# Second mixture: slots' outcome and result in two parts of columns, 256 and 128

## The chip, the core and the metric

The kernel runs on one core of a Trainium2 chip. Its time is counted in microseconds (us) of the device for one execution. A core has TensorE (PE, whose weight loads are listed apart as PEld), VectorE (DVE), ScalarE (ACT), GpSimd (POOL) and SyncE (SP, which here only issues transfers), and 16 DMA engines that move data between HBM and the core's memory. TensorE's products go to PSUM, in banks of 512 float32 columns; ACT and DVE copy them from there to SBUF.

## What is computed

A linear-attention recurrence gives 3072 rows of 384 numbers. A first mixture sends each row through one of eight experts. A second mixture, with which this case deals, collects the rows in 32 slots (8 experts with 4 slots each), runs each slot through its expert, and gives every row a weighted sum of the 32 slots' outcomes:

```python
def _moe2_ref(x, phi, w1, w2):
    logits = x @ phi
    ...
    slot_input = d.T @ x
    slot_input = slot_input.reshape(E, S_per_e, D)
    for e in range(E):
        h = np.maximum(slot_input[e] @ w1[e], 0.0)
        slot_out[e] = h @ w2[e]
    slot_out = slot_out.reshape(n_slots, D)
    c = logits - logits.max(1, keepdims=True)
    c = np.exp(c)
    c /= c.sum(1, keepdims=True) + 1e-09
    return (c @ slot_out).astype(np.float32)
```

Here D is 384, E is 8, S_per_e is 4 and the hidden size is 1024. w1 and w2 of this mixture are called v1 and v2 in the kernel.

## The kernel before

The span falls into three stretches: the attention (to about 110 us), the first mixture (to about 290 us), and the second mixture's end, which is all that the change touches.

The weights v1 and v2 are 32 tiles of 768 KB, fetched in a fixed order by SP: sixteen tiles of v1, then sixteen of v2 (`VORD`). They go wherever room comes free. The last eight tiles of v2, `V[2, 1, 0]` to `V[2, 1, 7]`, take the slots of tiles of v1, so SP waits until the hidden layer has read those (L215).

`experts` is the stage of the slots. The experts are in two groups of four (g = 0, 1), and the four of one group work side by side on TensorE, each in its own 32 columns of the array. `first(g, n)` computes half n of the hidden layer (L215) and ACT applies relu (L217). `turn(g, n)` transposes it in four blocks (L224), and DVE copies them out (L225). `last(g, n)` multiplies by four tiles of v2 and adds into the one bank `sop`, 384 columns (L233): for each tile four instructions side by side, which are a quad below; float32 products run as two passes over the columns, so that a tile costs two quads in the trace, and a call of `last` eight. Every one of the sixteen tiles of v2 must be in before `sop` is complete. Then ACT copies `sop` to `sst`, rounded (L256), and DVE adds what the rounding lost in other rows (L257).

`weights` makes the combining weights of 1024 rows on DVE and ACT, and `turned` (called by `ctt(c)`) transposes those of 512 rows on TensorE (L289) for ACT to copy to `ct` (L290).

`combine` makes the result. For c = 0 to 5, each standing for 512 rows, and for b = 0 to 3, one matmul multiplies `ct` by `sst` (L298: 128 rows of 384 columns), ACT or DVE copies it to `ob` (L300, L302), and SP writes `ob` out. For c = 0 there are three writes (L304 twice with one b each, L305 with two); for the others one of 768 KB (L305). A row of the result is 1536 bytes in a piece, and so are the packets of these writes. `ctt(c + 2)` follows each `combine(c)`.

The engines PE, DVE, ACT and POOL run in the order in which the code is written (`manual_schedule`), each on its own; waits between them are put in where one needs another's result or buffer.

Of the kernel before, what the change touches and what calls it, by code (L numbers as in the profile page):

```python
# [19 lines left out]
P = 128  # L20
# [184 lines left out]
def experts(nc, cn, ew, ez, pe, spx, rw, V, after=lambda blk: None):  # L205
    ident = cn["ident"]
    hs, ht = {}, {}

    def first(g, n, between=lambda: None):
        if n == 0:  # L210
            hs[g] = ew.tile([P, 2, HF], F32, tag="hs", bufs=1, name=f"hs{g}")
        hp = pe.tile([P, HF], F32, tag="h", name=f"ehp{g}_{n}")
        for k in range(3):
            for j in range(4):
                nc.tensor.matmul(hp[32 * j : 32 * j + 32, :], spx[:, g, k, j, :], V[1, 4 * g + j, n][:, k, :], start=(k == 0), stop=(k == 2))  # L215
        between()
        nc.scalar.activation(hs[g][:, n, :], hp, AF.Relu, scale=rw.scale[:, 0:1])  # L217

    def turn(g, n):
        if n == 0:  # L220
            ht[g] = ew.tile([P, 8, P], F32, tag="ht", bufs=2, name=f"ht{g}")
        tp = pe.tile([P, 4, P], F32, tag="a", name=f"htp{g}_{n}")
        for f in range(4):
            nc.tensor.transpose(tp[:, f, :], hs[g][:, n, f * P : (f + 1) * P], ident)  # L224
        nc.vector.tensor_copy(  # L225
            ht[g][:, 4 * n : 4 * n + 4, :].rearrange("p f (j q s) -> p (f j) q s", j=4, q=4),
            tp.rearrange("p f (j o s) -> p (f j) o s", j=4, o=4)[:, :, 0:1, :].to_broadcast([P, 16, 4, 8]),
        )

    def last(g, n):  # L230
        for f in range(4 * n, 4 * n + 4):
            for j in range(4):
                nc.tensor.matmul(sop[32 * j : 32 * j + 32, :], ht[g][:, f, 32 * j : 32 * j + 32], V[2, g, f][:, j, :], start=(g == 0 and f == 0), stop=(g == 1 and f == 7))  # L233

    sop = pe.tile([P, DM], F32, tag="so", name="sop")
    first(0, 0)
    after(0)
    first(0, 1)
    after(1)
    turn(0, 0)  # L240
    first(1, 0, lambda: turn(0, 1))
    after(2)
    first(1, 1)
    after(3)
    last(0, 0)
    turn(1, 0)
    turn(1, 1)
    after(4)
    last(0, 1)
    after(5)  # L250
    after(6)
    last(1, 0)
    after(7)
    last(1, 1)
    sst = ez.tile([P, DM], F32R, name="sst")
    nc.scalar.copy(sst, sop)  # L256
    nc.vector.scalar_tensor_tensor(sst, sst.bitcast(F32), rw.low[:, 0:1], sop, op0=ALU.mult, op1=ALU.add)  # L257
    return sst


def weights(nc, lp, ez, lt, p, cx=None):
# [21 lines left out]
    return cx
# [9 lines left out]
def combine(nc, po, pool, tag, bufs, sst, ct, c, out):  # L293
    ob = pool.tile([P, B, DM], F32, tag=tag, bufs=bufs, name=f"ob{c}")
    o = out.rearrange("(b c t) d -> c t b d", b=B, c=NC_)[c]
    for b in range(B):
        op = po.tile([P, DM], F32, tag="o", name=f"op{c}_{b}")
        nc.tensor.matmul(op, ct[:, b, :], sst, start=True, stop=True)  # L298
        if b % 2 == (c > 0):
            nc.scalar.copy(ob[:, b, :], op)  # L300
        else:
            nc.vector.tensor_copy(ob[:, b, :], op)  # L302
        if c == 0 and b < 2:
            nc.sync.dma_start(out=o[:, b : b + 1], in_=ob[:, b : b + 1])  # L304
    nc.sync.dma_start(out=o if c else o[:, 2:4], in_=ob if c else ob[:, 2:4])  # L305


def second(tc, cn, dsb, lt, v1, v2, out):
    nc = tc.nc
    with tc.tile_pool(name="ew", bufs=1) as ew, tc.tile_pool(name="vp", bufs=1) as vp, tc.tile_pool(name="pe", bufs=1, space=PSUM) as pp:  # L310
        pe = Banks(a=[(pp, "a", 2)], so=[(pp, "so", 1)], h=[(pp, "h", 2)], o=[(pp, "o", 3)])
# [161 lines left out]
def tile_main(ctx, tc, rk, kv, wu, wcat, phi, w1, w2, v1, v2, r_in, k_in, v_in, w_in, u_in, wcn, out, dbg=None, force=False):  # L473
# [874 lines left out]
    if True:  # L1348
# [314 lines left out]
```

## Time and profile before

| | us |
|---|---|
| median of 3 runs | 350.69 (348.82 to 350.75) |
| the profiled execution, its device time | 347.19 |
| the span of its trace | 345.1 |
| TensorE, busy | 321.6 (93%) |
| VectorE, busy | 228.9 (66%) |
| ScalarE, busy | 159.5 (46%) |
| HBM read and written | 74.49 MB and 10.10 MB, 245 GB/s over the span |

Times in the trace count from the span's start. A row of the timeline gives start, duration, engine, line, operation, what is written and read, and in brackets the idle time before it and what ended it. A row of windows gives, for a stretch, each engine's busy time and instructions, the clock granted to TensorE as a share of full speed, the mean busy share of the 16 DMA engines (it can pass 1, since packets overlap), and the GB/s that they moved. Busy shares over the whole span say little here: only the last 40 us are touched.

### The profile page before, as it was taken

How to read it: one execution, taken by the hardware profiler on the slowest of the kernel's cores; microseconds unless marked ns; L12 is line 12 of the kernel's file. 1: busy time of each engine (PE TensorE's matmuls, PEld its weight loads, DVE VectorE, ACT ScalarE, POOL GpSimd, SP SyncE). 2: the span in 40 equal slices, each digit the busy share in tenths (PEclk: the TensorE clock that was granted, in tenths of full speed). 3: DMA queues.
4: the chain of work that ended last, by engine and by line, in shares of the span. 5: the costliest groups of instructions: out<-in, count | busy, mean ns of one | idle time of the engine just before them, and what ended most of it. 6: DMA issues, size and time to landing. Idle time of an engine off the chain costs nothing. (4 is left out here: it accounts for less than half of the span.)

```text
span 345.1 us, 10483 instructions
## 1 busy us (share of the span) xinstructions
PE 321.6 (93%) x4351; PEld 262.9 (76%) x4351; DVE 228.9 (66%) x512; ACT 159.5 (46%) x351; POOL 139.5 (40%) x181
## 2 busy tenths in 40 slices
PE   8999997999998998999999999999999999999850
PEld 8666785777766683999999999998999998634440
DVE  6657688696978966776674847675685846417650
ACT  2344452445543545554655546564655543221360
POOL 4867684686843554804323242525224102200000
PEclk9999998999999999999999999999999999999995
DMA  7996567485777965898788787778866649479496
GB/s 230 293 242 206 166 201 228 128 283 184 236 230 243 385 229 185 265 308 312 262 284 289 247 272 267 264 270 274 317 189 225 225 128 330 151 268 371 142 349 206
DMA packets 45735, 85.29 MB, mean 247 GB/s; under 512 B 3838, under 2 KB 26672, under 8 KB 45680
## 3 DMA queue, kind: packets, MB, share of 16 engines
q1 hardware_dynamic: 43024, 80.63, 70.9%
q0 software_dynamic: 2128, 3.74, 4.0%
q8 instruction: 36, 0.59, 0.7%
q10 hardware_dynamic: 528, 0.16, 0.2%
q14 instruction: 19, 0.16, 0.1%
HBM read 74.49 MB, written 10.10 MB: 245 GB/s over the span
## 5 line engine op out<-in xcount | busy, mean ns | idle before, releaser
L1259 PE MATMUL hp<-xhl,wa 128*128 128x240 f32 x192 | 46.1, 282 | 0.2 <-issue 0.2
L996 DVE TENSOR_TENSOR wa<-w,wa 128x768 fp32r<-128x768 f32 x32 | 30.5, 956 | 22.4 <-ACT wa L1008 22.0
L1284 PE MATMUL yp<-wb,hh 128*128 128x384 f32 x128 | 45.2, 353 | 0.0
L1260 PE MATMUL hp<-xhl,wa 128*128 128x240 f32 x192 | 44.6, 275 | 0.0
L1285 PE MATMUL yp<-wb,hh 128*128 128x384 f32 x128 | 43.0, 336 | 0.0
L1286 PE MATMUL yp<-wb,hl 128*128 128x384 f32 x128 | 42.9, 335 | 0.0
L1190 POOL DMA_INDIRECT xg<-x_d,idg x16 | 19.8, 1238 | 50.7 <-DVE x L1292 38.1
L630 POOL TENSOR_TENSOR pd<-rkb 112x512 f32<-112x512 f32 x24 | 31.0, 1293 | 22.4 <-PE ud L658 17.1
L1314 POOL DMA_INDIRECT lt_d<-lsr,ids x16 | 17.7, 1107 | 50.5 <-ACT xhl L1249 28.4
L1259 PEld LDWEIGHTS hp<-xhl,wa 128*128 128x128 f32 x192 | 36.2, 189 | 0.5 <-ACT dsbv L135 0.5
L1260 PEld LDWEIGHTS hp<-xhl,wa 128*128 128x128 f32 x192 | 36.2, 189 | 0.0
L706 DVE COPY_PREDICATED at<-ih,ud 128x512 f32<-128x512 int32 x24 | 17.7, 738 | 26.7 <-ACT us L687 16.5
L996 DVE TENSOR_TENSOR wb<-w,wb 128x768 fp32r<-128x768 f32 x32 | 30.5, 953 | 2.0 <-ACT wb L1008 1.7
L1008 ACT CAST wb<-w 128x768 fp32r<-128x768 f32 x32 | 26.8, 838 | 9.5 <-PE yp L1286 5.5
L1269 ACT ACTIVATE hh<-hp 128x480 fp32r<-128x480 f32 x32 | 18.3, 572 | 21.9 <-PE hp L1262 19.3
L745 PE MATMUL yp<-at,kvt 64*48 64x64 f32 (+3 forms) x800 | 26.6, 248 | 1.4 <-DVE at L706 0.8
L1270 DVE SCALAR_TENSOR_TENSOR hl<-hp,hh 128x480 fp32r<-128x480 f32 x32 | 20.9, 655 | 9.6 <-ACT hh L1269 9.2
L1008 ACT CAST wa<-w 128x768 fp32r<-128x768 f32 x32 | 26.9, 840 | 0.0
L1284 PEld LDWEIGHTS yp<-wb,hh 128*128 128x128 f32 x128 | 24.0, 188 | 3.5 <-issue 3.5
L1262 PE MATMUL hp<-xhl,wa 128*128 128x240 f32 x192 | 26.7, 275 | 0.0
L745 PEld LDWEIGHTS yp<-at,kvt 64*48 64x48 f32 (+1 forms) x800 | 21.1, 122 | 7.3 <-PE wp L499 2.2
L648 PE MATMUL sc<-rks 48*64 48x128 f32 (+1 forms) x768 | 21.9, 250 | 4.6 <-DVE at L697 4.6
(346 smaller groups left out, 697.7 us busy)
## 6 DMA issues: line engine op xcount, KB each, us to landing
w<-in_w_dram SPq DMA_DIRECT2D x32, 768.0 KB
v<-in_v_dram SPq DMA_DIRECT2D x29, 768.0 KB
rkb<-in_rk_dram SPq DMA_DIRECT2D x24, 448.0 KB
kvt<-in_kv_dram SPq DMA_DIRECT2D x24, 384.0 KB
x_d<-x SPq DMA_DIRECT2D x5, 768.0 KB
out_dram<-ob SPq DMA_DIRECT2D x5, 768.0 KB
x<-in_v_dram SPq DMA_DIRECT2D x2, 768.0 KB
x_d<-x SPq DMA_DIRECT2D x2, 384.0 KB
```

Source lines behind the costliest of these rows:

```text
L630: nc.gpsimd.tensor_mul(t["pd"], rkt[:, 0], rkt[:, 1])
L648: nc.tensor.matmul(sc[c0 : c0 + HT, g, blocks(p, z), :], ks[r0 : r0 + D, p, HT * z : HT * z + HT], rs[r0 : r0 + D, p, HT * z :], start=Tru ...
L745: nc.tensor.matmul(d, kvt[s0 : s0 + HT, 1, h * D : h * D + m], w, start=(c == ph == z == 0), stop=(ph == z == 1))
L996: nc.vector.tensor_sub(lv, sl, hv.bitcast(F32))
L1008: nc.scalar.copy(hv, sl)
L1259: nc.tensor.matmul(hp[:, f, 0:ROOM], hi[:, k, fs], xh[:, k, 0:ROOM], start=(k == 0 and f == 0), stop=False)
L1260: nc.tensor.matmul(hp[:, f, 0:ROOM], lo[:, k, fs], xh[:, k, 0:ROOM], start=False, stop=False)
L1262: nc.tensor.matmul(hp[:, f, 0:ROOM], hi[:, k, fs], xl[:, k, 0:ROOM], start=False, stop=(k == 2 and f == 1))
L1270: nc.vector.scalar_tensor_tensor(l, p, 0.0, h.bitcast(F32), op0=ALU.max, op1=ALU.subtract)
L1284: nc.tensor.matmul(YP[e][bl], hh[:, f, bs], hi[:, f, :], start=st, stop=False)
L1285: nc.tensor.matmul(YP[e][bl], hh[:, f, bs], lo[:, f, :], start=False, stop=False)
L1286: nc.tensor.matmul(YP[e][bl], hlo[:, f, bs], hi[:, f, :], start=False, stop=en)
```

## The change

`experts` becomes a class, `Slots`, whose calls the kernel now writes out one by one. `last(i, g, n)` and `rows(i)` work on a part i of the columns: part 0 has columns 0 to 255, part 1 has 256 to 383, each with a bank and an `sst` of its own. All sixteen tiles of v2 are multiplied for part 0 first. The products for part 1 follow in four calls between the combines of part 0. `combine` takes a part: a bank of 512 columns holds two b of part 0 or four b of part 1, and is copied at once. The engine of each copy is given by a letter, "a" or "v". Each of the six `ob` has a buffer of its own; part 0 of an `ob` is written out when it is copied, and part 1 later. The end of `weights` for the last 1024 rows moves behind the first two combines. There are 13 writes in place of 8, of 1024 or 512 bytes in a piece.

```diff
-    def last(g, n):
+    def last(self, i, g, n):
+        c0, c1 = self.parts[i]
+        if (g, n) == (0, 0):
+            self.so[i] = self.pe.tile([P, c1 - c0], F32, tag=f"so{i}", name=f"sop{i}")
         for f in range(4 * n, 4 * n + 4):
             for j in range(4):
-                nc.tensor.matmul(sop[32 * j : 32 * j + 32, :], ht[g][:, f, 32 * j : 32 * j + 32], V[2, g, f][:, j, :], start=(g == 0 and f == 0), stop=(g == 1 and f == 7))
...
+                self.nc.tensor.matmul(self.so[i][32 * j : 32 * j + 32, :], self.ht[g][:, f, 32 * j : 32 * j + 32], self.V[2, g, f][:, j, c0:c1], start=(g == 0 and f == 0), stop=(g == 1 and f == 7))
+
+    def rows(self, i):
+        so = self.so[i]
+        c0, c1 = self.parts[i]
+        sst = self.ez.tile([P, c1 - c0], F32R, name=f"sst{i}")
+        self.nc.scalar.copy(sst, so)
+        self.nc.vector.scalar_tensor_tensor(sst, sst.bitcast(F32), self.rw.low[:, 0:1], so, op0=ALU.mult, op1=ALU.add)
+        return sst
...
-def combine(nc, po, pool, tag, bufs, sst, ct, c, out):
-    ob = pool.tile([P, B, DM], F32, tag=tag, bufs=bufs, name=f"ob{c}")
+def combine(nc, po, sst, ct, ob, c, part, out, engines, early=False):
+    c0, c1 = part
+    w = c1 - c0
+    n = min(B, 512 // w)
     o = out.rearrange("(b c t) d -> c t b d", b=B, c=NC_)[c]
-    for b in range(B):
-        op = po.tile([P, DM], F32, tag="o", name=f"op{c}_{b}")
-        nc.tensor.matmul(op, ct[:, b, :], sst, start=True, stop=True)
-        if b % 2 == (c > 0):
-            nc.scalar.copy(ob[:, b, :], op)
-        else:
-            nc.vector.tensor_copy(ob[:, b, :], op)
-        if c == 0 and b < 2:
-            nc.sync.dma_start(out=o[:, b : b + 1], in_=ob[:, b : b + 1])
-    nc.sync.dma_start(out=o if c else o[:, 2:4], in_=ob if c else ob[:, 2:4])
+    for q, eng in zip(range(0, B, n), engines):
+        op = po.tile([P, n, w], F32, tag="o", name=f"op{c}_{c0}_{q}")
+        for b in range(n):
+            nc.tensor.matmul(op[:, b, :], ct[:, q + b, :], sst, start=True, stop=True)
+        (nc.scalar.copy if eng == "a" else nc.vector.tensor_copy)(ob[:, q : q + n, c0:c1], op)
+        if early:
+            nc.sync.dma_start(out=o[:, q : q + n, c0:c1], in_=ob[:, q : q + n, c0:c1])
+    if not early:
+        nc.sync.dma_start(out=o[:, :, c0:c1], in_=ob[:, :, c0:c1])
...
+        CX.append(weights(nc, lp, ez, lt, 1, ltf[:, 0:1024].bitcast(F32R).rearrange("p (n s) -> p n s", n=8))())
+        ctt(0)
+        sl.last(0, 1, 0)
+        ctt(1)
+        cx2 = weights(nc, lp, ez, lt, 2, x2f[:, 0:1024].bitcast(F32R).rearrange("p (n s) -> p n s", n=8))
+        sl.last(0, 1, 1)
+        sst.append(sl.rows(0))
...
+        sl.last(1, 0, 0)
+        out_of(0, 0, "va", True)
+        out_of(0, 1, "va")
+        CX.append(cx2())
+        ctt(2)
+        out_of(0, 2, "aa")
+        sl.last(1, 0, 1)
+        ctt(3)
+        out_of(0, 3, "av")
+        sl.last(1, 1, 0)
+        ctt(4)
+        out_of(0, 4, "av")
+        sl.last(1, 1, 1)
+        sst.append(sl.rows(1))
+        ctt(5)
+        out_of(0, 5, "va")
         for c in range(NC_):
-            combine(nc, po, wr, "wr", NWR, sst, CT[c], c, out)
-            if c + 2 < NC_:
-                ctt(c + 2)
+            out_of(1, c, "va"[c % 2])
```

On TensorE, before, the last tile of v2 (`v2_1_7`) is followed at once by the combines; `sop` is the slots' bank, `ctp` a transposition of combining weights, `op1_2` the product for c = 1 and b = 2, and the numbers at the end of a name count tiles:

```order
L233 MATMUL sop_4837<-v2_1_6_4833,x2_2810 32x384 x4
L233 MATMUL sop_4837<-v2_1_7_4835,x2_2810 32x384 x4
L298 MATMUL op0_0_5033<-sst_5029,ct0_4984 128x384
L298 MATMUL op0_1_5037<-sst_5029,ct0_4984 128x384
L298 MATMUL op0_2_5041<-sst_5029,ct0_4984 128x384
L298 MATMUL op0_3_5044<-sst_5029,ct0_4984 128x384
L289 MATMUL ctp2_5048<-ident_160,ltt_199 128x128 x4
```

In the changed kernel, at the same place, four tiles of group 0 are multiplied again for part 1 (`sop1`) before the first combine; `op0_0_2` is c = 0, columns from 0, b from 2:

```order
L241 MATMUL sop0_4917<-v2_1_6_4833,x2_2810 32x256 x4
L241 MATMUL sop0_4917<-v2_1_7_4835,x2_2810 32x256 x4
L241 MATMUL sop1_5030<-v2_0_0_4570,x2_2810 32x128 x4
L241 MATMUL sop1_5030<-v2_0_1_4631,x2_2810 32x128 x4
L241 MATMUL sop1_5030<-v2_0_2_4678,x2_2810 32x128 x4
L241 MATMUL sop1_5030<-v2_0_3_4680,x2_2810 32x128 x4
L297 MATMUL op0_0_0_5047<-sst0_5022,ct0_4973 128x256 x2
L297 MATMUL op0_0_2_5052<-sst0_5022,ct0_4973 128x256 x2
```

The last tile of v2 is still the last thing that the slots' bank waits for; only the width has changed, and eight quads of part 1 stand between it and the first combine.

Further on TensorE, before, transposition and combine alternate; c = 2 to c = 4:

```order
L298 MATMUL op2_3_5085<-sst_5029,ct0_4984 128x384
L289 MATMUL ctp4_5089<-ident_160,x2_2810 128x128 x4
L298 MATMUL op3_0_5096<-sst_5029,ct3_5068 128x384
L298 MATMUL op3_1_5099<-sst_5029,ct3_5068 128x384
L298 MATMUL op3_2_5102<-sst_5029,ct3_5068 128x384
L298 MATMUL op3_3_5105<-sst_5029,ct3_5068 128x384
L289 MATMUL ctp5_5109<-ident_160,x2_2810 128x128 x4
```

In the changed kernel, the stretch from the combine of c = 3 to that of c = 4:

```order
L297 MATMUL op3_0_2_5115<-sst0_5022,ct3_5104 128x256 x2
L241 MATMUL sop1_5030<-v2_1_0_4821,x2_2810 32x128 x4
L241 MATMUL sop1_5030<-v2_1_1_4823,x2_2810 32x128 x4
L241 MATMUL sop1_5030<-v2_1_2_4825,x2_2810 32x128 x4
L241 MATMUL sop1_5030<-v2_1_3_4827,x2_2810 32x128 x4
L285 MATMUL ctp4_5136<-ident_160,x2_2810 128x128 x4
L297 MATMUL op4_0_0_5142<-sst0_5022,ct3_5104 128x256 x2
L297 MATMUL op4_0_2_5146<-sst0_5022,ct3_5104 128x256 x2
```

The transposition for c now stands directly ahead of the combine of the same c, and the products of part 1 stand ahead of both; before, a whole combine of another c stood between a transposition and its use.

## Rows read from the trace of the kernel before

**Rows 1.** Windows over the end of the span; columns as described above.
```profile
305.00:322.00 17.00, 17.00 (x173) 6.81 (x169) 9.85 (x23) 3.48 (x7) 0.00 (x0) 1.00 1.06 376
322.00:324.00 2.00, 2.00 (x25) 0.67 (x24) 1.83 (x6) 0.69 (x2) 0.00 (x0) 1.00 0.30 100
324.00:326.00 2.00, 0.99 (x12) 0.16 (x8) 0.63 (x2) 0.48 (x1) 0.00 (x0) 1.00 0.00 0
326.00:328.00 2.00, 1.70 (x11) 1.66 (x12) 1.29 (x4) 1.11 (x3) 0.00 (x0) 1.00 0.00 0
328.00:330.00 2.00, 2.00 (x16) 1.93 (x15) 1.88 (x4) 2.00 (x6) 0.00 (x0) 1.00 0.94 325
330.00:334.00 4.00, 2.89 (x16) 2.05 (x15) 3.16 (x7) 3.72 (x9) 0.00 (x0) 1.00 1.03 366
334.00:336.00 2.00, 0.00 (x0) 0.00 (x0) 0.00 (x0) 0.00 (x0) 0.00 (x0) 0.86 1.03 353
336.00:341.00 5.00, 0.00 (x0) 0.00 (x0) 0.00 (x0) 0.00 (x0) 0.00 (x0) 0.50 1.04 352
341.00:343.00 2.00, 0.00 (x0) 0.00 (x0) 0.00 (x0) 0.00 (x0) 0.00 (x0) 0.50 0.31 108
343.00:345.10 2.10, 0.00 (x0) 0.00 (x0) 0.00 (x0) 0.00 (x0) 0.00 (x0) 0.50 0.00 0
```

**Rows 2.** Timeline from the last tiles of v2 to the second combine.
```profile
322.67 0.13 PEld L233 LDWEIGHTS sop<-v,x 128*32 128x32 f32 x4 [0.19 <-issue]
322.99 0.13 PEld L233 LDWEIGHTS sop<-v,x 128*32 128x32 f32 x4 [0.19 <-issue]
...
324.20 0.16 PEld L233 LDWEIGHTS sop<-v,x 128*32 128x32 f32 x8 [0.76 <-DMA v<-in_v_dram]
325.12 0.48 ACT L256 CAST sst<-sop 128x384 fp32r<-128x384 f32 x1 [2.44 <-PE sop L233]
325.64 0.61 DVE L257 SCALAR_TENSOR_TENSOR sst<-sst,rlow,sop 128x384 fp32r<-128x384 f32 x1 [1.37 <-ACT sst L256]
...
326.31 0.97 PE L298 MATMUL op<-sst,ct 128*128 128x384 f32 x4 [1.25 <-DVE sst L257]
326.78 0.86 ACT L300 COPY ob<-op 128x384 f32<-128x384 f32 x2 [1.18 <-PE op L298]
...
327.12 0.60 PE L289 MATMUL ctp<-ident,ltt 128*128 128x128 f32 x4
327.29 0.83 SPq L304 DMA_DIRECT2D out_dram<-ob  x2
```

**Rows 3.** Groups by line, 290 to 346 us: busy us, mean ns of one.
```profile
L302 DVE COPY ob<-op 128x384 f32<-128x384 f32 x12 | 6.1, 553 | 1.3 <-PE op L298 1.1
...
L290 ACT CAST ct<-ctp 128x512 fp32r<-128x512 f32 x6 | 3.6, 617 | 0.1
L225 DVE COPY x<-htp 128x512 f32<-128x512 f32 x4 | 2.7, 686 | 7.2 <-PE htp L224 7.2
L1476 PE MATMUL lgq<-x2t,ph 128*32 128x128 f32 x12 | 1.5, 274 | 0.0
```

**Rows 4.** DMA queues, 329 to 336 us (writes): packets, MB, share of 16 engines.
```profile
q1 hardware_dynamic: 1703, 2.52, 102.6%
```

**Rows 5.** DMA queues, 0 to 2.9 us: ACT's loads, nearly all of 1024 bytes.
```profile
q10 hardware_dynamic: 128, 0.11, 11.6%
```

**Rows 6.** DMA queues, 3 to 6 us: ACT's loads of 128 bytes in a piece.
```profile
q10 hardware_dynamic: 400, 0.05, 10.7%
```

More of the change, by code (lines that the diff above doesn't have):

```diff
@@ L202, in vload, with __init__, first @@
     return t
[L205 to L209, printed above, removed]
+class Slots:
+    def __init__(self, nc, cn, ew, ez, pe, spx, rw, V, parts=((0, DM),)):
+        self.nc, self.ident, self.ew, self.ez, self.pe, self.spx, self.rw, self.V, self.parts = nc, cn["ident"], ew, ez, pe, spx, rw, V, parts
+        self.hs, self.ht, self.so = {}, {}, {}
+    def first(self, g, n, between=lambda: None):
+        nc = self.nc
@@ L236, in experts @@
[L236 to L258, printed above, removed]
+                self.nc.tensor.matmul(self.so[i][32 * j : 32 * j + 32, :], self.ht[g][:, f, 32 * j : 32 * j + 32], self.V[2, g, f][:, j, c0:c1], start=(g == 0 and f == 0), stop=(g == 1 and f == 7))
@@ L322, in second @@
             if c % 2 == 0:
-                cx = weights(nc, ew, ew, lt, c // 2)
+                cx = weights(nc, ew, ew, lt, c // 2)()
             turned(nc, cn, pe, cx, c, ct[:, c])
-        sst = experts(nc, cn, ew, ew, pe, spx, rw, V)
+        sl = Slots(nc, cn, ew, ew, pe, spx, rw, V)
+        for g in range(2):
+            for n in range(2):
+                sl.first(g, n)
+            for n in range(2):
+                sl.turn(g, n)
+            for n in range(2):
+                sl.last(0, g, n)
+        sst = sl.rows(0)
         for c in range(NC_):
-            combine(nc, pe, ew, "ob", 3, sst, ct[:, c], c, out)
+            combine(nc, pe, sst, ct[:, c], ew.tile([P, B, DM], F32, tag="ob", bufs=3, name=f"ob{c}"), c, (0, DM), out, "avav")
 def general(tc, cn, dp, r_in, k_in, v_in, w_in, u_in, wcn, phi, w1, w2, v1, v2, out):
@@ L1582, in ctt, with out_of @@
+            CT.append(ctt.t[:, c % 3])
             turned(nc, cn, po, CX[c // 2], c, CT[c])
+        def out_of(i, c, engines, early=False):
+            combine(nc, po, sst[i], CT[c], ob[c], c, parts[i], out, engines, early)
         lp = Views(ls.rearrange("p a b -> p (a b)"))
-        CX = []
-        sst = experts(nc, cn, ew, ez, po, spx, rw, V, after)
+        CX, sst = [], []
+        sl = Slots(nc, cn, ew, ez, po, spx, rw, V, parts)
+        sl.first(0, 0)
+        sl.first(0, 1)
+        sl.turn(0, 0)
@@ new lines, in tile_main @@
+        sl.first(1, 0, lambda: sl.turn(0, 1))
+        sl.first(1, 1)
+        CX.append(weights(nc, lp, ez, lt, 0)())
+        sl.last(0, 0, 0)
+        sl.turn(1, 0)
+        sl.last(0, 0, 1)
+        sl.turn(1, 1)
+        CX.append(weights(nc, lp, ez, lt, 1, ltf[:, 0:1024].bitcast(F32R).rearrange("p (n s) -> p n s", n=8))())
[4 more added lines that the diff above has]
+        sl.last(0, 1, 1)
```

73 lines of the change are left out of this document (36 added, 37 removed).

## The prediction

> **What bounds the kernel now.** I read the table of windows over the last 40 us first, because only that end is touched. From 305 to 322 us the DMA engines are full (share 1.06, 376 GB/s) with the last tiles of v2, and they run dry in the next 2 us [rows 1]. TensorE then shows what ended last: its quads stand 0.32 us apart, but those of the last tile start at 324.20 only, after 0.76 us of waiting for that tile's transfer [rows 2]. So the loads set when the slots' sums are complete. From there a chain of single steps follows: the quads to about 325.1, ACT's copy at 325.12, DVE's correction at 325.64, the first combine at 326.31, its copy at 326.78, the first write at 327.29 [rows 2]. Nothing moves on the DMA engines between 324 and 328. From 328 they are full again: 0.94, 1.03, 1.03 and 1.04 up to 341 us, a thin rest that ends before 343, and 2.1 us to the span's end. The compute engines stop by 334 [rows 1]. The end is thus the moment at which the writing starts plus the time that 4.72 MB (3072 rows of 1536 bytes) need on full DMA engines. Combines and copies have 7 us to spare; they only have to stay ahead of the writing.
>
> **The start of the writing.** The change can't start it before the last tile of v2: part 0 also sums over all sixteen tiles, and the loads, their order and what they wait for are the same. What it saves is width. A quad of 384 columns takes 0.32 us, one of 256 takes 2/3 of it; the last tile's two quads save 0.21. ACT's copy took 479 ns at 384 columns [rows 2] and 617 at 512 [rows 3], about 1.08 ns a column, so 256 columns take 0.34 and save 0.14. DVE's copies, 553 ns at 384 and 686 at 512 [rows 3], give 1.04 ns a column, so the correction saves 0.13. The combine can start at 326.31 - 0.48 = 325.83. TensorE is free by then: the eight quads of part 1 go in from 324.20 + 0.43 = 324.63. The trace has no quad of 128 columns. The nearest row is a matmul of 32 array columns and 128 data columns, 12 in 1.5 us with 0.27 for the last [rows 3], so 0.11 apart; the other bound is the 0.32 of 384 columns. I take 0.11, since it has the same width and the same weights' shape: 8 x 0.11 = 0.9, done at 325.5. (At 0.32 they end at 327.2, and the start is 1.2 later than before.) The first write now needs two matmuls of 256 columns (+0.07) and a DVE copy of 512 columns, 0.69 in place of ACT's of 384, 0.48: from combine to write 0.98 becomes 1.26, and it goes out at 327.1. **Start: -0.2 us.**
>
> **The price of smaller pieces.** From a queue's row, share x 16 engines x window / packets is the time of one packet. The writes of 1536 bytes: 1.026 x 16 x 7 / 1703 = 67 ns [rows 4], 68 without the small completion packets. Packets of 860 bytes on average: 0.116 x 16 x 2.9 / 128 = 42 ns [rows 5]. Of about 125 bytes: 0.107 x 16 x 3 / 400 = 13 ns [rows 6]. On the line through the last two, about 0.040 ns a byte over 8, a packet of 1024 bytes takes 48.5, one of 512 takes 28, and one of 1536 would take 69, as measured. Each DMA engine wrote 192 pieces of 1536 bytes in 192 x 68 = 13.06 us. It now writes 192 of 1024 and 192 of 512: 9.3 + 5.4 = 14.7 us. **Smaller pieces: +1.65 us.** The bounds are 0 (the same per byte, 23 ns for 512 bytes) and, at 68 ns for every packet, 192 x 40 = +7.7 and 192 x 20 = +3.8 more. The interpolation lies between measured sizes, so I take it.
>
> The Trainium skill ("DMA: Bandwidth & Descriptors", section "Why small descriptors are slow (HBM only)") puts a fixed cost of about 3 cycles on each packet beside one cycle for 32 bytes. By that, 512 bytes cost 19 cycles against 51 for 1536, and the same term would be an estimated +0.8 us; the rows show a larger fixed share.
>
> **Whether the writing stays fed.** Before, it was: six combines lie inside 7 us against 13 us of writing. Now TensorE has 24 more quads of part 1 between the combines of c = 2 and c = 5, and the transposition for c stands directly ahead of its own combine. One round for c = 3, 4 or 5 is a chain through two engines: eight quads 0.9, four transpositions 0.60 [rows 2], ACT's copy to `ct` 0.62 [rows 3], the four matmuls of the combine 0.5 (at 384 columns the next work on TensorE began 0.81 after them, 326.31 to 327.12 [rows 2]; two thirds of it), handovers 0.05: 2.6 to 2.7 us. What a round hands over, 512 KB of part 0, is 32 packets per DMA engine, 1.55 us. So the writing runs dry once per round. In order: the writes of c = 0 leave at 327.1 and 327.5, that of c = 1 at 327.9. c = 2 is held by ACT, which copies a half each of c = 0 and c = 1 (0.62 each), then `ct`, then both halves of c = 2, back to back from 326.6: 330.4. Then 332.75, 335.5 (a copy on DVE ends it) and 338.15 for c = 3, 4, 5 (c = 3 a little sooner, since TensorE starts its round at 329.0, while ACT still copies c = 2). Bytes flow 0.8 us after a write is issued: 327.29 to about 328.1, which leaves 0.94 of the first 2 us [rows 1]; now from 327.9. The queue is empty from 331.0 to 331.2, 332.75 to 333.55, 335.1 to 336.3, and 337.85 to 338.95. **Pauses: 0.2 + 0.8 + 1.2 + 1.1 = +3.3 us.** Part 1 then follows from 338.7 on, a copy of 0.69 on two engines by turns, which is 0.35 per write against 0.9 of writing, so no more pauses. The bounds: 0, if ACT and TensorE overlap better than I have them, and at 0.32 us per quad 1.7 more in each of three rounds, +8.4.
>
> DVE's moved work, the end of `weights` (0.42 to 0.69 each, some 2.5 us), lies behind c = 1's copy and is done by 330.4, while the transposition that needs it comes after 332; it costs nothing, and 1 us of it would show only if it ran past 332. SP issues 13 writes at 0.4 each; all lie beside the copies.
>
> **The last engine.** Before, most DMA engines end near 341.15 (328.1 + 13.06), and a few go on; their share of 0.31 in 341 to 343, with nothing after [rows 1], lets me put the last bytes at 342.8. In pauses the late ones catch up, so I take this rest in proportion to the last unbroken stretch, 7 us instead of 13: 0.9 for 1.65. **-0.75 us.**
>
> **Sum.** -0.2 + 1.65 + 3.3 - 0.75 = +4.0 us: bytes end at 346.8 in place of 342.8, the span at 349.1 and the profiled time at 351.2. The profiled execution (347.19) is 3.5 below the median of the runs shown (350.69); I add the difference to the median: 354.7.
>
> **Rivals.**
> - *The writing stays fed.* If copies keep ahead, only start, pieces and tail count: between +0.7 (with the tail's gain) and +1.45, 351.8. For it: ACT and DVE had 7 us to spare. Against it: the chain of a round counts, not the engines' sum.
> - *Not slower: the uneven tail goes.* A pause lets the late engines catch up, so all 1.65 us of the rest in 341 to 343 may go, and the start is 0.2 earlier. That decides once pieces and pauses cost less than 1.85 together, for which small packets must cost about as much per byte as large ones and the rounds must take under 2 us. With 1 us of pauses: 349.8. Against it: rows 5 and 6 put a fixed cost on a packet.
> - *Quads of 128 columns are slow.* Loading weights takes as long as such a quad; if the two don't overlap, a quad is 0.22 and each round 0.9 longer: +2.7 and about 0.5 at the start, 358. If TensorE's clock fell to its lower level in the gaps, as it did once TensorE stopped (0.86 in 334 to 336, then 0.50) [rows 1], the price is like it; it stayed at 1.00 through the half-idle 324 to 328.
> - *Each transfer brings its own pause.* Five more writes at 0.76 us each: +3.8 beyond the sum, 358.5. Against it: eight writes ran at 1.03 without a gap. The Trainium skill ("DMA: Bandwidth & Descriptors", section "Bandwidth") advises batches of 1 MiB and over; by that rule the change, which goes from 768 KB to 512 and 256 KB, would lose. The trace does not show it for queued transfers, which overlap.
>
> **How the numbers follow.** Sum 0.55, fed writing 0.20, tail 0.07, slow quads 0.13, a pause per write 0.05. A measurement of this kernel can tell about 1% (3.5 us) from no change, so slower begins at 354.2. The sum's own range is 353 to 357; about two thirds of its chance lie above 354.2. Slower: 0.37 + 0.13 + 0.05 = 0.55. Same: 0.18 + 0.20 and most of 0.07, 0.42; faster 0.03. The range leaves out the tail's case and the upper half of the slow cases: 351.7 to 358.5.
>
> **What would show it.** In the trace after: the first write near 327.1; packets of 512 bytes near 28 ns; four dips of the DMA share between 330 and 339; writes of c = 3, 4, 5 about 2.6 us apart; last bytes near 346.8. A DMA share at 1.0 without dips from 328 on would make the pauses wrong; a first write well before 326 would make the first step wrong.

## The result and the profile after

| | before | after |
|---|---|---|
| median, same chip, in turns | 349.75 us (348.62 to 350.75) | 355.64 us (353.84 to 355.99) |
| the profiled execution, its device time | 347.19 us | 355.93 us |
| the span of its trace | 345.1 us | 354.2 us |
| TensorE, VectorE, ScalarE busy | 321.6, 228.9, 159.5 us | 328.3, 229.7, 160.7 us |

The changed kernel is slower: its time is 1.0144 of that before, with a 95% interval of 1.0105 to 1.0184. In every ratio here, runs more than 1.5% above the fastest of the same kernel are left out. The ratio makes the loss 5.0 us (3.7 to 6.4), the medians of four runs each make it 5.9, and 4.0 were forecast. The time of 355.64 lies in the range given, 0.9 above the forecast of 354.7.

The two profiled executions differ by more, 8.7 us, and part of that is no work of the change. Between 54 and 66 us, far ahead of the changed code, the clock granted to TensorE fell in both kernels, but for longer in the execution of after; there it fell again between 132 and 136 us, where it stayed at 1.00 before. Windows of before, then of after (the last three figures are the granted clock, the DMA share and the GB/s):

```profile
54.00:58.00 4.00, 2.71 (x64) 2.63 (x64) 3.96 (x10) 0.37 (x1) 0.25 (x1) 0.69 0.98 289
58.00:62.00 4.00, 4.00 (x48) 2.09 (x45) 0.76 (x2) 1.33 (x3) 1.47 (x2) 0.88 0.16 39
```

```profile
58.00:62.00 4.00, 4.00 (x21) 1.58 (x20) 2.13 (x3) 0.74 (x2) 1.27 (x1) 0.50 0.27 64
62.00:66.00 4.00, 3.96 (x93) 2.94 (x93) 1.44 (x3) 1.86 (x4) 2.03 (x3) 0.80 0.13 17
...
132.00:136.00 4.00, 3.86 (x31) 1.28 (x31) 1.93 (x11) 3.13 (x6) 0.24 (x1) 0.59 0.43 124
```

By the first product of the second mixture's hidden layer (L215 before, L219 after) the execution of after is 3.47 us late: 303.37 against 299.90 us. So nothing below compares absolute times. The zero is either that product, called **H**, or the start of the last tile's quads for part 0, called **T**. T comes 24.31 us after H before, 24.48 after. The last bytes of the result leave 42.86 us after H before and 48.28 after: the changed stretch costs 5.42 us in the profiles.

The windows over the end of after stand against [rows 1]; T is at 327.85:

```profile
322.00:324.00 2.00, 1.84 (x28) 0.73 (x20) 1.74 (x6) 1.11 (x3) 0.00 (x0) 1.00 1.07 376
324.00:326.00 2.00, 0.53 (x12) 0.16 (x8) 1.35 (x3) 0.42 (x1) 0.00 (x0) 1.00 0.92 319
326.00:328.00 2.00, 0.60 (x12) 0.15 (x8) 0.00 (x0) 0.00 (x0) 0.00 (x0) 1.00 0.06 21
...
332.00:334.00 2.00, 2.00 (x40) 1.66 (x40) 1.64 (x4) 1.07 (x2) 0.00 (x0) 1.00 1.02 337
334.00:336.00 2.00, 1.33 (x23) 0.96 (x24) 0.32 (x1) 1.14 (x2) 0.00 (x0) 1.00 1.03 342
336.00:338.00 2.00, 1.33 (x29) 0.89 (x21) 0.37 (x1) 0.62 (x2) 0.00 (x0) 1.00 0.52 164
338.00:340.00 2.00, 2.00 (x40) 1.67 (x40) 0.69 (x1) 0.85 (x2) 0.00 (x0) 1.00 0.47 158
340.00:342.00 2.00, 1.32 (x12) 1.09 (x11) 0.87 (x2) 0.88 (x3) 0.00 (x0) 1.00 0.78 262
342.00:344.00 2.00, 2.00 (x20) 2.00 (x20) 1.59 (x4) 1.44 (x3) 0.00 (x0) 1.00 0.39 130
...
348.00:350.00 2.00, 0.00 (x0) 0.00 (x0) 0.00 (x0) 0.00 (x0) 0.00 (x0) 0.50 1.07 285
350.00:352.00 2.00, 0.00 (x0) 0.00 (x0) 0.00 (x0) 0.00 (x0) 0.00 (x0) 0.50 0.28 84
```

Where before the DMA share stands at 1.03 from the first bytes to the thin rest, here it is full for 4 us and then 0.52, 0.47, 0.78 and 0.39. The DMA engines wait for the combines. And when they are full again, at 348, they move 285 GB/s in place of 352: those are the pieces of 512 bytes.

From the single packets in the trace I counted three things for each kernel: **work** (the sum of the durations of the result's packets, completion packets left out, over 16 engines), **dry** (stretches of 0.1 us and more with fewer than four engines at work, the end left out), and **rest** (what the time from the first to the last bytes has beyond work and dry: the uneven end, above all).

| us | first bytes after T | work | dry | rest | last bytes after T |
|---|---|---|---|---|---|
| before | 3.94 | 13.53 | 0 | 1.08 | 18.55 |
| after | 3.80 | 15.18 | 3.66 | 1.16 | 23.80 |
| forecast, as a difference | -0.2 | +1.65 | +3.3 | -0.75 | +4.0 |
| difference | -0.14 | +1.65 | +3.66 | +0.08 | +5.25 |

The 5.25 us here and the 5.42 above differ by the 0.17 us by which T comes later after H.

**Start.** The timeline after, against [rows 2]:

```profile
327.85 1.24 PEld L241 LDWEIGHTS sop<-v,x 128*32 128x32 f32 x40 [1.88 <-DMA v<-in_v_dram]
327.85 1.51 PE L241 MATMUL sop<-v,x 128*32 128x256 f32 x40 [1.40 <-DMA v<-in_v_dram]
328.56 0.37 ACT L247 CAST sst<-sop 128x256 fp32r<-128x256 f32 x1 [2.72 <-PE sop L241]
328.96 0.48 DVE L248 SCALAR_TENSOR_TENSOR sst<-sst,rlow,sop 128x256 fp32r<-128x256 f32 x1 [3.58 <-ACT sst L247]
329.50 1.23 PE L297 MATMUL op<-sst,ct 128*128 128x256 f32 x8
...
330.76 0.97 SPq L300 DMA_DIRECT2D out_dram<-ob  x2
```

TensorE still waits for the last tile of v2, now 1.88 us in place of 0.76, since it is done sooner with the tile before. From T to the correction it takes 1.11 us (1.44 before), to the combine 1.65 (2.11), to the first write 2.91 (3.09). The eight quads of part 1 lie in the wait for ACT and DVE, as forecast.

**Rounds.** The stretch from the combine of c = 3 to that of c = 4:

```profile
334.90 0.74 PE L297 MATMUL op<-sst,ct 128*128 128x256 f32 x4 [0.67 <-ACT ct L286]
...
335.57 1.08 PE L241 MATMUL sop<-v,x 128*32 128x128 f32 x32
...
336.59 0.66 PE L285 MATMUL ctp<-ident,x 128*128 128x128 f32 x4
337.28 0.58 ACT L286 CAST ct<-ctp 128x512 fp32r<-128x512 f32 x1 [1.24 <-PE ctp L285]
...
337.92 0.74 PE L297 MATMUL op<-sst,ct 128*128 128x256 f32 x4 [0.67 <-ACT ct L286]
```

On the chain from one combine to the next, one thing follows the other without a gap: 0.67 us of combine, 1.02 of quads, 0.69 of transposition, 0.64 for ACT's copy and the handover, 3.02 in all. The writes of c = 2 to 5 are issued 5.69, 8.58, 11.60 and 14.47 us after T, so 2.9, 3.0 and 2.9 us apart, and a write of 512 KB holds the engines for 1.57 (32 packets of 49 ns). The DMA engines are dry for 0.94, 1.42 and 1.30 us between them.

### The profile page after: what moved, and what is told of

It reads as the page before. It is cut to its first block, busy times and chain, and to the rows that moved or that the text cites. A ratio compares the mean times of both kernels' runs of the same rounds, so it can differ in the third digit from the quotient of the medians.

```text
span 354.2 us, 10792 instructions
## 1 busy us (share of the span) xinstructions
PE 328.3 (93%) x4503; PEld 268.6 (76%) x4503; DVE 229.7 (65%) x509; ACT 160.7 (45%) x350; POOL 139.6 (39%) x181
## 4 chain that ended last, share of the span: by engine, by line
PE 76%; DVE 14%; DMA 4%; ACT 2%; POOL 1%; issue 1%; DVEq 0%; ACTq 0%
PE yp L1289 7%; PE yp L1290 6%; PE yp L1291 6%; PE hp L1264 6%; PE hp L1267 6%; PE hp L1265 6%; DMA v<-in_v_dram 4%; PE lgt L834 3%; PE yp L750 3%; PE ehp L219 3%; PE wp L504 3%; DVE at L711 2%; PE trp L761 2%; PE sc L653 2%; PE ud L676 2%; PE op L297 2%
## 5 line engine op out<-in xcount | busy, mean ns | idle before, releaser
L653 PE MATMUL sc<-rks 48*64 48x128 f32 (+1 forms) x768 | 21.1, 247 | 4.6 <-DVE at L702 4.6
```

The source lines that it names most:

```text
L653: nc.tensor.matmul(sc[c0 : c0 + HT, g, blocks(p, z), :], ks[r0 : r0 + D, p, HT * z : HT * z + HT], rs[r0 : r0 + D, p, HT * z :], start=Tru ...
```

## The experiments

My theory was that of the forecast: smaller pieces cost 1.65 us, and the rest of the loss is that each combine of c = 3 to 5 waits for a chain on TensorE and ACT. The rivals: quads of 128 columns are slow in themselves, or each further write brings its own pause. In this section "dry", "rest", T and H are used as above; ratios are to the kernel before, with 95% intervals.

### The products of part 1 taken out of the rounds

Three of the four calls of `last` for part 1 move ahead of the last four tiles of part 0, where TensorE waits for loads.

```diff
+        sl.last(1, 0, 0)
         ctt(1)
+        sl.last(1, 0, 1)
+        sl.last(1, 1, 0)
         ...
         sl.last(0, 1, 1)
         sst.append(sl.rows(0))
         ...
-        sl.last(1, 0, 0)
+        sl.last(1, 1, 1)
         out_of(0, 0, "va", True)
         ...
         out_of(0, 2, "aa")
-        sl.last(1, 0, 1)
         ...
         out_of(0, 3, "av")
-        sl.last(1, 1, 0)
         ...
         out_of(0, 4, "av")
-        sl.last(1, 1, 1)
```

> The changed kernel with the products of part 1 taken out of the rounds: three of their four calls run while TensorE waits for the last tiles of v2, the fourth right after the last tile. Transpositions stay where the change put them. Measured in the trace from the start of the last tile's quads for part 0 to the last bytes written: 18.6 us in the kernel before, 24.0 in the changed one. Theory (the writing runs dry because a round of products, transposition, copy and combine takes 2.9 us against 1.55 of writing): a round falls by the 1.0 us of its eight quads to about 2.0, the stretch to 21.0, the time to 0.85% below the changed kernel's, that is 0.6% above before. Rival (the writing stays fed, the loss is in small pieces alone): the stretch stays at 24.0, 1.4% above before. Rival (a pause for each write): 24.0 as well.

Measured: ratio 1.0008 [0.9968, 1.0048]; rounds of 2.04, 1.86 and 1.71 us; dry 0.54 us in place of 3.66; last bytes 20.72 us after T (21.0 expected). Windows, with T at 326.31:

```profile
332.00:334.00 2.00, 1.18 (x8) 0.94 (x8) 0.90 (x2) 1.32 (x3) 0.00 (x0) 1.00 1.03 343
334.00:336.00 2.00, 1.18 (x8) 0.94 (x8) 0.85 (x2) 1.40 (x4) 0.00 (x0) 1.00 0.92 309
336.00:338.00 2.00, 1.78 (x16) 1.78 (x16) 1.32 (x3) 0.91 (x3) 0.00 (x0) 1.00 0.85 288
338.00:340.00 2.00, 1.59 (x15) 1.45 (x13) 1.47 (x3) 1.39 (x3) 0.00 (x0) 1.00 0.92 303
```

The DMA share that stood between 0.39 and 0.78 is now between 0.85 and 1.03. Of the 5.25 us this one move gives back 3.08. T comes 24.50 us after H, so the moved quads cost nothing where they went: TensorE waits for the loads there. The ratio is lower than the 1.006 expected, and its interval leaves that out. The last bytes come 45.22 us after H, 2.36 later than before, which would be 1.007; no run shows why the times say less.

### The transpositions one combine earlier

```diff
         out_of(0, 0, "va", True)
+        ctt(2)
         out_of(0, 1, "va")
         CX.append(cx2())
-        ctt(2)
+        ctt(3)
         out_of(0, 2, "aa")
         sl.last(1, 0, 1)
-        ctt(3)
+        ctt(4)
         out_of(0, 3, "av")
         ...
-        ctt(4)
+        ctt(5)
         out_of(0, 4, "av")
         ...
-        ctt(5)
```

> The changed kernel with each transposition of combining weights from c = 2 on moved one combine ahead, so that its copy on ACT lies beside other work; the products of part 1 stay in the rounds. Theory (a round is a chain through TensorE and ACT): a round falls from 2.9 to what TensorE alone needs, 0.67 + 1.0 + 0.45 = 2.1 us, the stretch from the last tile to the last bytes from 24.0 to about 21.0, the time to 0.6% above before. If the products were the whole cause, rounds would stay near 2.9 and the stretch at 24.0. Rival (small pieces alone): 24.0.

Measured: ratio 1.0087 [1.0053, 1.0120]; last bytes 23.41 us after T, a miss by 2.4. The first write left 4.27 us after T in place of 2.9. Windows around T, which is at 326.62:

```profile
322.00:324.00 2.00, 0.95 (x16) 0.16 (x8) 1.90 (x5) 0.36 (x1) 0.00 (x0) 1.00 1.07 373
324.00:326.00 2.00, 0.64 (x8) 0.16 (x8) 0.15 (x1) 0.42 (x1) 0.00 (x0) 0.86 0.35 119
326.00:328.00 2.00, 1.38 (x20) 0.89 (x24) 0.00 (x0) 0.23 (x1) 0.00 (x0) 0.50 0.00 0
328.00:330.00 2.00, 2.00 (x31) 1.56 (x24) 0.48 (x1) 0.14 (x1) 0.00 (x0) 0.50 0.00 0
```

TensorE's clock fell from 2.4 to 1.2 GHz (1.00 to 0.50) just as the last tile came, after 4 us in which it was busy for 0.95 and 0.64 of 2 us. So the run mixed two things, and I ran the same kernel again.

> The kernel of transposes_ahead again: each transposition one combine earlier, the products of part 1 left where they are. If its late first write (4.27 us after the last tile) came from the lower granted clock of TensorE in that profile alone, a profile with the clock at 1.00 has the first write at 2.9 and the last bytes at 21 to 22; if the clock falls again at the same place, about 4.3 and 23.4, and the order itself brings it.

Measured: ratio 1.0076 [1.0045, 1.0107]; the clock fell again, for a shorter time:

```profile
324.00:326.00 2.00, 0.64 (x8) 0.16 (x8) 1.13 (x3) 0.42 (x1) 0.00 (x0) 1.00 0.80 275
326.00:328.00 2.00, 0.65 (x8) 0.40 (x12) 0.00 (x0) 0.00 (x0) 0.00 (x0) 0.78 0.06 15
328.00:330.00 2.00, 2.00 (x37) 1.39 (x28) 0.48 (x1) 0.37 (x1) 0.00 (x0) 0.50 0.00 0
```

The first write came 4.19 us after T, as in the second of the two cases expected; the last bytes, at 22.49, lie between the two. The quads from T on, two of part 0 and eight of part 1, took 1.51 us in after and take 2.79 in both profiles here, so that the first combine starts 2.72 us after T in place of 1.65. From the second profile:

```profile
327.35 2.79 PE L241 MATMUL sop<-v,x 128*32 128x256 f32 x40 [1.41 <-DMA v<-in_v_dram]
...
334.99 0.63 PE L285 MATMUL ctp<-ident,x 128*128 128x128 f32 x4 [1.05 <-DVE x L276]
```

With the clock back at 1.00, the last two rounds (to the writes of c = 4 and 5) are 2.07 and 1.59 us against 3.0 and 2.9, and dry is 1.10 in place of 3.66. So the transposition's place is part of the round's length. The round ahead of them is still 2.78: the transposition for c = 4, now ahead of the combine of c = 3, waits 1.05 us for DVE's end of `weights` (the second row), a wait that the expectation didn't have. Whether this order brings the fall of the clock stays open: up to T its instructions are those of after, whose TensorE was as idle (0.53 and 0.60 of 2 us) and kept its clock in its one profile.

### Both moves together

The products as in the first experiment, the transpositions for c = 2 and 3 ahead of the last tiles, those for c = 4 and 5 between the combines of c = 3 and 4.

```diff
+        sl.last(1, 0, 0)
         ctt(1)
+        sl.last(1, 0, 1)
+        sl.last(1, 1, 0)
+        ctt(2)
+        ctt(3)
         cx2 = weights(nc, lp, ez, lt, 2, x2f[:, 0:1024].bitcast(F32R).rearrange("p (n s) -> p n s", n=8))
         sl.last(0, 1, 1)
         ...
         out_of(0, 3, "av")
-        sl.last(1, 1, 0)
         ctt(4)
+        ctt(5)
         out_of(0, 4, "av")
         ...
```

> The changed kernel with both causes of the long rounds taken out: the products of part 1 as in products_early, and the transpositions for c = 2 and 3 ahead of the last tile, those for c = 4 and 5 two combines ahead. Theory (start -0.2, smaller pieces +1.6, pauses 0): the stretch from the last tile to the last bytes is that of before_split_columns, about 20.0 us, and the time 0.4% above before. Rival (something else in the order of parts costs time, besides pauses and pieces): it stays at the 20.7 of products_early or above.

Measured: ratio 1.0068 [1.0029, 1.0107]; no dry stretch; last bytes 20.48 us after T.

```profile
332.00:334.00 2.00, 1.76 (x16) 1.53 (x13) 0.44 (x2) 1.53 (x3) 0.00 (x0) 1.00 1.02 345
334.00:336.00 2.00, 1.45 (x13) 1.25 (x12) 1.84 (x4) 0.93 (x4) 0.00 (x0) 1.00 1.03 340
336.00:338.00 2.00, 1.68 (x16) 1.54 (x14) 1.56 (x3) 1.39 (x3) 0.00 (x0) 1.00 1.03 334
```

The share stays at 1.02 and above. All 3.66 us of pauses are gone, and what is left against before, 1.93 us after T, is the pieces' 1.73 (work 15.26) with the rest of 1.44 in place of 1.08, less the start's 0.16. The two moves are not additive: once the products are out, only half a microsecond of pauses remains for the transpositions. Its ratio is no better than that of the products alone, though its last bytes are 0.24 us earlier after T; T itself came 0.32 us later after H (24.82 against 24.50), so that counted from H the last bytes come alike, at 45.30 and 45.22 us. The intervals of the two ratios overlap.

### The pieces alone, and the number of writes alone

Both are the kernel before with 14 writes in place of 8: the first cuts each write, but the first two, in columns 256 and 128, the second by rows.

```diff
-    nc.sync.dma_start(out=o if c else o[:, 2:4], in_=ob if c else ob[:, 2:4])
+    for c0, c1 in ((0, 256), (256, DM)):
+        nc.sync.dma_start(out=(o if c else o[:, 2:4])[:, :, c0:c1], in_=(ob if c else ob[:, 2:4])[:, :, c0:c1])
```

> The kernel before with every write but the first two cut in two by columns, 256 and 128, so in pieces of 1024 and 512 bytes; 14 writes in place of 8. Nothing else differs. Theory (a piece of 1024 bytes costs 48 ns, one of 512 some 29, against 68 for 1536): the writing takes 11/12 of 192 x 9 ns = 1.6 us longer, the stretch from the last tile to the last bytes 20.2 in place of 18.6, the time +0.45%. Rival (small pieces carry the whole loss): 24.0, +1.4%. Rival (pieces cost nothing per byte): 18.6, 0%.

```diff
-    nc.sync.dma_start(out=o if c else o[:, 2:4], in_=ob if c else ob[:, 2:4])
+    for b in (0, 2) if c else (2, 3):
+        w = 2 if c else 1
+        nc.sync.dma_start(out=o[:, b : b + w], in_=ob[:, b : b + w])
```

> The kernel before with every write but the first two cut in two by b, so that the pieces stay 1536 bytes; 14 writes in place of 8. Theory (queued writes overlap, a write as such costs nothing here): the stretch stays 18.6 us, the time within 0.1% of before. Rival (each write brings its own pause of 0.8 us): 6 x 0.8 = 4.8 us more, +1.4%.

Measured: cut in columns, ratio 1.0035 [0.9997, 1.0073], work 15.16, last bytes 20.10 us after T, 1.55 later than before. Cut by rows, ratio 1.0037 [0.9995, 1.0080], work 13.34, last bytes at 18.62, 0.07 later. The two ratios can't be told apart, nor from 1, but the stretches can. The queues' rows show why. After, first in a stretch of 1024 bytes, then in one of 512 (packets, MB, share of 16 engines):

```profile
q1 hardware_dynamic: 1039, 1.03, 102.3%
```

```profile
q1 hardware_dynamic: 2217, 1.10, 103.0%
```

The first is of 333 to 336 us, the second of 346 to 350. Cut in columns, of 340 to 344 us, and cut by rows, of 331 to 336:

```profile
q1 hardware_dynamic: 1750, 1.24, 103.8%
```

```profile
q1 hardware_dynamic: 1262, 1.81, 102.6%
```

Share x 16 x window / packets, the small completion packets (32, 61, 57, 82) left out, gives 49 ns for 1024 bytes, 31 for 512, 39 for the mixture and 70 for 1536; [rows 4] gives 70 by the same working. Thus the size of the pieces costs 1.6 us, and the number of writes, at 0.07, nothing that shows.

### Loading earlier

The tiles that TensorE waits for can come sooner: two of the last eight tiles of v2 go to buffers that are free already.

```diff
-        for k in vit:
-            V[k] = vload(nc, vx, "vx", NVX, k, v1, v2)
+        for i, k in enumerate(vit):
+            V[k] = vload(nc, wr, "wr", NWR, k, v1, v2) if i < 2 else vload(nc, vx, "vx", NVX, k, v1, v2)
         ...
```

In the changed kernel, where buffers of `ob` move besides, and in the one before:

> The changed kernel with one thing else: two of the last eight tiles of v2 go into two buffers that are free before the hidden layer starts, so that the DMA engines, idle for some 5 us there, fetch them then; the buffers of four ob move for it. Measured from the first product of the hidden layer to the last tile's quads for part 0 (24.3 us before, 24.5 in the changed kernel), and to the last bytes (42.9 and 48.3). Theory (the first write can't start sooner, because the last tile's arrival sets it): with the last tile some 4 us sooner part 0 is complete at about 20.5, limited by TensorE, and the last bytes come at 20.5 + 23.8 = 44.3, still 0.4% above before. Rival (the start hangs on something else, on TensorE or DVE): 24 and 48 as in the changed kernel.

> The kernel before with the same two tiles fetched early, nothing else. Theory: with 384 columns TensorE itself needs nearly all of the 24.3 us, since it waited only 0.8 us for the last tile; 23.6 us to the last tile's quads, 42.1 to the last bytes, the time 0.2% below before. Rival (the loads alone set it): 20.5 and 39, 1.1% below before.

Measured in the changed kernel: ratio 1.0050 [1.0020, 1.0080]; T comes 20.86 us after H in place of 24.48, but the first write 3.70 us after T in place of 2.90. Last bytes 45.44 us after H, expected 44.3. (This profiled execution took 358.09 us, the longest of its twelve, but the clock in the stretch is 1.00, and the next kernel, profiled at 349.07 us, gives the same T and first write.) In the kernel before: ratio 0.9995 [0.9958, 1.0032], T 24.06 us after H in place of 24.31, last bytes 42.58 after H. The windows from H to T, of the changed kernel and of the one before, both with early loads (TensorE's busy time comes first):

```profile
308.33:329.19 20.86, 20.86 (x242) 9.07 (x244) 9.66 (x26) 4.54 (x8) 2.40 (x3) 1.00 0.74 250
```

```profile
303.55:327.61 24.06, 24.06 (x242) 9.07 (x245) 12.71 (x34) 4.86 (x9) 2.40 (x3) 1.00 0.64 218
```

TensorE is busy all the time in both. With 384 columns it needs nearly all of the 24.31 us by itself; the narrower products are what lets part 0 use the earlier loads. That is the one gain that the change really opens: 3.2 us at T against the kernel before with the same loads. Neither step brings it alone: narrower products moved T by +0.17 us, earlier loads by -0.25, both together by -3.45.

### Early loads with whole rows at the end

This kernel has the early loads, writes c = 4 and 5 whole (rows of 1536 bytes), and has the products of part 1 nearer to the start (`None` makes a combine without a write of its own). The diff leaves out the loads, shown above.

```diff
         ctt(2)
-        out_of(0, 2, "aa")
         sl.last(1, 0, 1)
+        out_of(0, 2, "aa")
         ctt(3)
-        out_of(0, 3, "av")
         sl.last(1, 1, 0)
+        out_of(0, 3, "av")
+        sl.last(1, 1, 1)
+        sst.append(sl.rows(1))
+        ctt(4)
+        for c in range(4):
+            out_of(1, c, "va"[c % 2])
+        ctt(5)
+        for c in (4, 5):
+            out_of(0, c, "av", None)
+            out_of(1, c, "va"[c % 2], None)
+            nc.sync.dma_start(out=out.rearrange("(b c t) d -> c t b d", b=B, c=NC_)[c], in_=ob[c])
```

> A version meant to beat both: loads_early, with the transpositions ahead of a call of products, part 0 written first for c = 0 to 3 alone, part 1 of these next, and c = 4 and 5 last in whole rows of 1536 bytes. Theory: start at 20.5 + 3.8 = 24.3 us after the first product of the hidden layer, writing 6.2 + 3.6 + 4.4 us with about 0.8 of pauses and 1.0 of unevenness at the end, last bytes at about 40.3 in place of 42.9, the time 0.7% below before. If pauses of 2 us or more remain, no gain.

Measured: ratio 0.9982 [0.9952, 1.0012]; last bytes 42.54 us after H, expected 40.3. T comes at 20.86 again, and the first write is again late, at 3.70. The timeline shows by what:

```profile
323.63 0.41 DVE L258 TENSOR_REDUCE cm<-lte 128x8 f32<-128x256 f32 x1
324.08 0.42 DVE L260 TENSOR_TENSOR ls<-lte,cm 128x256 f32<-128x256 f32 x1
324.54 0.42 ACT L261 ACTIVATE ls<-ls 128x256 f32<-128x256 f32 x1 [1.82 <-DVE ls L260]
324.86 0.35 ACT L247 CAST sst<-sop 128x256 fp32r<-128x256 f32 x1
325.25 0.48 DVE L248 SCALAR_TENSOR_TENSOR sst<-sst,rlow,sop 128x256 fp32r<-128x256 f32 x1 [0.74 <-ACT sst L247]
```

T is at 323.34, so the sums could be copied at about 324.05 (0.71 after T, as in after). ACT first does the exponential of `weights`, for which it waited 1.82 us on DVE, and DVE was busy with `weights` up to then. The 0.8 us are that work: once the loads are early, DVE is the limit. The writing was dry for 1.16 us besides.

### Feeding the writing all the time

The next two kernels have that work of `weights` behind the first combines, all four calls of `last` for part 1 between the combines of c = 1 and 3 or right behind, and c = 4 and 5 whole. The second places the work of `weights` earlier again; the diff is from the first to the second:

```diff
         out_of(0, 1, "va")
+        cx2 = weights(nc, lp, ez, lt, 2, x2f[:, 0:1024].bitcast(F32R).rearrange("p (n s) -> p n s", n=8))
         sl.last(1, 0, 0)
-        out_of(0, 2, "va")
+        out_of(0, 2, "av")
+        CX.append(cx2())
         sl.last(1, 0, 1)
-        out_of(0, 3, "va")
+        out_of(0, 3, "aa")
         sl.last(1, 1, 0)
-        cx2 = weights(nc, lp, ez, lt, 2, x2f[:, 0:1024].bitcast(F32R).rearrange("p (n s) -> p n s", n=8))
         sl.last(1, 1, 1)
         sst.append(sl.rows(1))
-        CX.append(cx2())
+        ctt(4)
         ...
```

> The changed kernel with the two early loads, and an order in which the writing should never wait: the transpositions for c = 2 and 3 stand ahead of the first combine, c = 0 to 3 of part 0 follow with three of the four product calls of part 1 between them, the whole end of weights lies behind DVE's copies of c = 3, and c = 4 and 5 are written whole. Theory (pauses and piece size are the whole loss, and the delay of the first write in loads_early came from DVE's weights): first write 2.9 us after the last tile (3.70 in loads_early); full rows cost 68 ns and split ones 49 + 30, so four split c cost about 4 x 0.35 = 1.4 us beyond whole rows and the writing takes about 14.5 us; no stretch with the DMA engines dry (at most 0.3 us in all); last bytes 19.0 to 19.8 us after the last tile, 39.9 to 40.9 after the first product of the hidden layer against 42.6 to 42.9 of before; ratio 0.993 (0.990 to 0.996). Rival (the engines' uneven end or the widths' cost eats it): dry time under 0.5 us but last bytes over 20.5 after the last tile, ratio 0.996 to 1.001.

> fed_writing with its two dry stretches shortened: in its profile the DMA share fell to 0.15 in one microsecond ahead of the first write of part 1 and to 0.34 in one ahead of the write of c = 4, because the end of weights came only after DVE's copies of c = 3. Here the first half of that work stands behind c = 1 and the rest behind c = 2, the copies of c = 3 are both on ACT, the transposition for c = 4 fills TensorE's wait for the second part's rows, and the copies of part 1 alternate between DVE and ACT. Theory (the writing's dry stretches and the piece size are the whole loss): the dry stretch ahead of part 1 stays (TensorE's 32 quads of part 1 and their rows end about 8 us after the last tile, 0.8 us late), the one ahead of c = 4 goes: first write 2.9, write of c = 4 about 12 (14.75 before), last bytes 20.0 to 20.8 after the last tile, 40.8 to 41.7 after the first product of the hidden layer against 42.6 to 42.9 of before; ratio 0.993 to 0.998. Rival (the uneven end of the engines grows by as much as the pauses shrink): write of c = 4 at 12, last bytes still over 21.5, ratio 0.998 to 1.002.

Measured for the first: ratio 0.9995 [0.9962, 1.0028]; first write 2.88 us after T, so the delay was DVE's; but dry 1.04 us ahead of part 1 and 0.84 ahead of the write of c = 4, and last bytes 22.17 us after T, 43.03 after H:

```profile
336.00:337.00 1.00, 0.97 (x9) 0.83 (x8) 0.93 (x3) 1.00 (x3) 0.00 (x0) 1.00 0.15 51
...
341.00:342.00 1.00, 0.00 (x0) 0.00 (x0) 0.39 (x1) 0.54 (x1) 0.00 (x0) 1.00 0.34 92
```

Ahead of part 1 the timeline has the four calls of `last`, 1.0 us each where I had counted 0.9, and behind them the second part's rows, ready only 8.8 us after T. Ahead of c = 4 the transpositions wait for DVE's end of `weights`:

```profile
337.39 1.09 PE L285 MATMUL ctp<-ident,x 128*128 128x128 f32 x8 [0.42 <-DVE x L276]
```

Its rest, 2.0 us, is also longer than in any other kernel (1.0 to 1.4): in its last 1.6 us packets of 65 ns come at the pace of a single DMA engine. Why that one is so late stays open. For the second: the pause ahead of c = 4 is gone (its write leaves 13.17 us after T, expected 12), that ahead of part 1 is still 1.16, the rest is 1.26; last bytes 20.82 us after T and 41.68 after H, 1.18 less than before. The ratio is 0.9970 [0.9931, 1.0008]. That is the best of the versions, and still no gain that the measurement shows.

## Why the prediction was right, and where it was off

**The number: nearer than the change.** 354.7 is 0.9 us below the 355.64 measured, but the change of +4.0 is 1.0 below the 5.0 of the ratio and 1.9 below the 5.9 of the medians. I had added it to 350.69, and the median before is 349.75 in the comparison; that difference of 0.94 helped by luck.

**What bounds the end: right.** Loads, then a chain of single steps, then the writing. Taking out most of the pauses (products moved, same pieces, same writes) moved the last bytes by 3.08 us. The ratio fell from 1.0144 to 1.0008, which is more than the 3.08 us explain; with no pauses left it was 1.0068. That the loads set T was only just true of the kernel before: with the loads earlier T moved by 0.25 us, since TensorE then has no idle time left.

**The start: right,** -0.14 at the first bytes and -0.18 at the first write for -0.2. T did not move by more than 0.17 us against H, as said: part 0 needs all tiles.

**Smaller pieces: the difference right, its exactness luck.** The pieces took 49 and 30 ns for the forecast 48.5 and 28, and the work grew by 1.65 us as forecast. But the writes of 1536 bytes take 70 ns and not 68: I had taken off too little for the 64 completion packets in [rows 4]. The work is 13.53 us before for the forecast 13.06, and 15.18 after for 14.7, about 0.5 more both times, and the two errors cancel. The kernel before with cut columns shows the same by itself: +1.63 of work and +1.55 at the last bytes. By the cost per packet in the Trainium skill ("DMA: Bandwidth & Descriptors", section "Why small descriptors are slow (HBM only)") the same term was an estimated +0.8; the runs show twice that, and the measurement decides.

**Pauses: the mechanism right, the size a little low,** 3.66 for 3.3. They are three and not four: the first, 0.2 us ahead of c = 2, didn't come, since its write left 5.69 us after T and not 6.2. The others are 0.94, 1.42 and 1.30 for 0.8, 1.2 and 1.1, since a round takes 2.9 to 3.0 us and not 2.6 to 2.7. The combine holds TensorE 0.67 us where I had 0.5 (I had scaled the time to the next work by the columns), eight quads 1.02 where I had 0.9, and the transposition 0.69 where I had 0.60.

**The last engine: wrong,** and the larger half of the miss. I let the uneven end shrink with the last unbroken stretch, by 0.75 us, on the idea that late engines catch up in pauses. The rest is 1.08 us before and 1.16 after. It is 1.01 with 16 us of unbroken writing (cut columns) and 1.18 with short pauses (products early). Over all kernels here it has no relation to the pauses. With this term at 0 the sum would have been +4.75, for 5.25 measured.

**The rivals.** *The writing stays fed* fell: three pauses of 0.9 to 1.4 us. *The uneven tail goes* fell with the last term. *Quads of 128 columns are slow* fell for the quads: eight in 1.02 us, 0.13 each, not 0.22. Its other half, a falling clock, did not come in after, but did in the two profiles of one experiment, where the quads from T on took 2.79 us in place of 1.51 and the first write came 1.3 us later. *Each transfer brings its own pause* fell: six more writes cost 0.07 us.

## What to carry to other kernels

Where a kernel ends in a write that fills the DMA engines, the work ahead of it only has to keep them fed, so count each chain of dependent steps against what one write takes, not the engines' busy shares. Cutting rows into parts is paid for twice, in packets (1.65 us here) and in steps between the writes (3.66 us, which another order removes). It gains only if the first write then starts sooner by more than that. Here two limits lay side by side at that start, TensorE's products and the loads, and taking away one of them alone moved it by at most 0.25 us.

## What I had not expected of the hardware

- The uneven end of the DMA engines is about as long for 13.5 us of unbroken writing as for writing with pauses: 1.0 to 1.4 us, in one run 2.0.
- With less work ahead of the last tile, TensorE waited longer for the same loads (1.88 us in place of 0.76). In both profiles of one kernel its clock then fell to 1.2 GHz just at the start of the chain on which the end hangs, and the first write came 1.3 us later; in the changed kernel, as idle there, it stayed at 2.4 GHz. What decides between the two stays open.
- Four times eight quads of 128 columns run at 0.13 us each in the middle of other work, close to the 0.11 of the matmuls in [rows 3].
